# An HGRN2 recurrence with a maxout feed-forward network: the first FFN group begun on half its tokens, and the first loads taken by four tokens and turned by products

## The chip, the cores and the metric

The kernel runs on one core of a Trainium2 chip. The metric is the device time in microseconds. A core has five engines with instruction streams of their own: PE (matrix products, with its weight loads shown apart as PEld), DVE (vector), ACT (scalar), POOL (GpSimd) and SP, which here only issues transfers. ACT issues some transfers too. All data are fp32 on the chip; the weights come as float64 and are rounded on the chip.

## The reference

```python
f = 1.0 / (1.0 + np.exp(-f_logit))
state = np.zeros((B, H, D, D))                 # B 4, H 8, S 768, D 48
for t in range(S):
    state = f[:, :, t, :, None] * state + np.einsum('bhd,bhe->bhde', k[:, :, t], v[:, :, t])
    y[:, :, t] = np.einsum('bhd,bhde->bhe', q[:, :, t], state)
x = y.transpose(0, 2, 1, 3).reshape(B * S, H * D)   # 3072 x 384
h = np.maximum(np.maximum(x @ w1, x @ w2), x @ w3)  # 384 -> 768
return h @ w_out                                    # 768 -> 384
```

## The kernel before

**Units.** The recurrence is cut into 24 units: unit u is chunk u // 2 of 64 time steps for two of the four batches, so it has 128 tokens. Four units make a group of 512 tokens for the FFN, and there are six groups. Inside a unit the recurrence is done by products: with r the decay from a step to the end of the chunk and prod the decay from its beginning, kh = k * r and qh = q * prod; the pairs kh x qh, masked to be causal, times v give the part inside the chunk, and qh times the carried state gives the rest.

**Feature-major layout.** The scans run along time, so f, k and q are needed with the features on the partitions: 48 features of a head padded to DP = 64, two heads (par) on 128 partitions. `load_tokens` (L156) fetches a unit with tokens on the partitions: one transfer for each of the two batches, whose contiguous pieces are one token of one head, 48 floats. `transposed` (L239) turns such a tile by four PE transposes of 128 x 128 against the identity. Units 0 to 7 (BY_ROWS) go this way; later ones come in 32 x 32 blocks that DVE turns (L246), and `pad_blocks` (L140) fills their padding on POOL. The padding holds 40 for f (so the gate is 1) and 0 for k and q.

**The work of a unit.** `sigmoids` (L257) turns f and makes the gate on ACT. `after` (L277) does the first scan (r, L282), a reciprocal, the turn of k and kh (L289). `before` (L294) does the second scan (prod, L296), the turn of q and qh (L300). `carry` (L303) scales the state on POOL. `keys` (L310) turns kh back (L315, copied by ACT at L317), `pairs` (L322) makes the scores (L328) and masks them on DVE (L331), `values` (L335) makes y (L342) and the new state (L351), which DVE adds (L359) or, for units 0 and 1, copies (L357). `finish` (L364) adds the carried part (L372) and ACT copies y into heads (L378). The product tiles of y have one buffer, those of the FFN (`p`) two; the turned k and q of units 0 to 3 also use the `p` buffers.

**The FFN.** `pack` (L382) gathers heads into xT by ten transfers (L389). `ffn` (L394) has 18 steps (six column blocks j, three weight matrices i), each three products of 512 columns (L401) into a `p` tile; the first of three is copied by ACT (L405), the other two go into a running maximum on DVE (L407). Then come four output steps (L422). It is a generator: `fill(n)` runs the next n steps between the parts of the units. A 512-column product shows as two records in the profile.

**Weights.** They come in 24 pieces of 384 KB (18 for the first layer, 6 for the second). A piece is rounded by two ACT operations (`round_begin`, L212 and L215), two on DVE and one on POOL (`round_middle`, L224, L225, L227) and a last on DVE (`round_end`, L234). Three pieces are ended before the first FFN step and the rest during the first group's steps.

**Order.** The order of all instructions is written out by hand (L459 to L583): each engine runs its own in that order, and SP's and ACT's transfers are issued in that order too. Units 0 to 3 come first; after them `busy(14)` (L448), 14 products whose result is not used, stands while xT is packed, and then the first group's FFN is interleaved with units 4 to 7, and so on. At the end, between the eighth and ninth step of the last group, the smallest decay is reduced (L578 to L582) to decide whether a general path must run.

Of the kernel before, what the change touches and what calls it, by code (L numbers as in the profile page):

```python
# [50 lines left out]
GATE_PAD = 40.0  # L51
# [3 lines left out]
def kernel(  # L55
# [32 lines left out]
    def fast():  # L88
        ctx = ExitStack()
        with ctx:  # L90
# [31 lines left out]
            for t in r_tiles:  # L122
                nc.gpsimd.memset(t[:, LEN:], 1.0)
            ones = keep.tile([128, 1], FP32, name="ones")
            nc.vector.memset(ones, 1.0)
# [5 lines left out]
            PADS = {"f": GATE_PAD, "k": 0.0, "q": 0.0}  # L131
            room = {nm: [keep.tile([128, 2 * H * DP], FP32, name=f"{nm}_ld{i}") for i in range(2)] for nm in PADS}
            rows = {nm: [room[nm][u // 2][:, u % 2 * H * DP:(u % 2 + 1) * H * DP].rearrange("t (h d) -> t h d", d=DP)
                         for u in range(4)] for nm in PADS}
            blocks = {nm: [t.rearrange("p (n h d) -> p n h d", n=C // 32, d=32) for t in room[nm]] for nm in PADS}
            for nm, pad in PADS.items():
                for t in rows[nm]:
                    nc.vector.memset(t[:, :, D:DP], pad)

            def pad_blocks(i):  # L140

                for nm, pad in PADS.items():
                    for p0 in (32, 96):
                        yield nc.gpsimd.memset(blocks[nm][i][p0:p0 + 32, :, :, D - 32:], pad)
# [9 lines left out]
            both = (nc.sync, nc.scalar)  # L154

# [6 lines left out]
            def load(u, queues=one, names="fkq"):  # L162
                for nm, src in (("f", f_logit), ("k", k), ("q", q)):
                    if nm not in names:
                        continue
                    if u < BY_ROWS:
# [12 lines left out]
            def load_v(u):  # L179
                load_tokens(v_tiles[u % NLD], v, u)  # L180
# [58 lines left out]
            def transposed(x, name="tr"):  # L239
                t = {"tr": ps_tr, "p": ps_f}[name].tile([128, HP, 128], FP32, name=name)  # L240
                flat = x.rearrange("t h d -> t (h d)")
                for hp in range(HP):
                    nc.tensor.transpose(t[:, hp, :], flat[:, hp * 128:(hp + 1) * 128], ident)  # L243
                return t.rearrange("p h (a t) -> p h a t", a=2)
# [5 lines left out]
            by_pair = lambda t: t.rearrange("p (a h) t -> p h a t", a=2)  # L250
# [6 lines left out]
            def sigmoids(u):  # L257
                gate = gate_tiles[u % 2]
                if u < BY_ROWS:
                    nc.scalar.activation(by_pair(gate)[:, :, :, 1:], transposed(rows["f"][u % 4]), AF.Sigmoid)  # L260
                else:
                    sig = work.tile([128, C // 32, 2 * HP, 32], FP32, name="sig")
                    nc.scalar.activation(sig, block("f", u), AF.Sigmoid)  # L263
                    ready[u] = sig

            def features(nm, u):

                if u < BY_ROWS:
                    t = transposed(rows[nm][u % 4], "p" if u < GRP else "tr")
                    return t.rearrange("p h a t -> p a h t")  # L270
# [6 lines left out]
            def after(u):  # L277
# [7 lines left out]
                nc.vector.reciprocal(from_inv[u % 2][:, :, 0], whole)  # L285
                kt = features("k", u)
# [48 lines left out]
            def values(u):  # L335
# [9 lines left out]
                if u < NU - 2:  # L345
# [10 lines left out]
                    if u < 2:  # L356
                        nc.vector.tensor_copy(new, ds)  # L357
# [24 lines left out]
            def pack(u0, u1, xT, queues=one):  # L382

                t, n = slice(u0 * UT, (u1 + 1) * UT), 0
                for h in range(H):
                    for lo, hi in ((h * D, min(h * D // 128 * 128 + 128, h * D + D)), (h * D // 128 * 128 + 128, h * D + D)):
                        if lo < hi:
                            p0 = h % 2 * DP + lo - h * D
                            queues[n % 2].dma_start(out=xT[lo % 128:lo % 128 + hi - lo, lo // 128, t],  # L389
# [3 lines left out]

            def ffn(g, xT):  # L394
                hm = work.tile([128, NJ, TOK], FP32, name="hm", bufs=1)
                for j in range(NJ):
                    top = None
                    for i in range(3):
                        p = ps_f.tile([128, TOK], FP32, name="p")
                        for kt in range(NK):  # L400
                            nc.tensor.matmul(p, lhsT=w_in[i][:, kt, j * 128:(j + 1) * 128], rhs=xT[:, kt, :],  # L401
                                             start=(kt == 0), stop=(kt == NK - 1))
                        if i == 0:
                            top = work.tile([128, TOK], FP32, name="top")
                            nc.scalar.copy(top, p)  # L405
                        else:
                            nc.vector.tensor_tensor(hm[:, j, :] if i == 2 else top, p, top, op=ALU.max)  # L407

                        if g == 0:
                            step, last = 3 * j + i, 3 * NJ  # L410
                            for r in range(*(3 + (len(pieces) - 3) * n // last for n in (step, step + 1))):
                                round_end(r)
                                if r + 2 < len(pieces):
                                    round_begin(r + 2)
                                    round_middle(r + 2)
                            load_weights(2, r + 1)
                            next(pads, None)
                        yield
                for i in range(GRP):
# [4 lines left out]
                    if g == 0:  # L424
                        next(pads, None)
# [3 lines left out]
                    for a in range(2):  # L429
                        t0 = (2 * bp + a) * S + c * C  # L430
                        nc.sync.dma_start(out=out[t0:t0 + C, :], in_=o[a * C:(a + 1) * C, :])
                    yield
# [18 lines left out]
            pads = iter(())  # L451

# [6 lines left out]
            with tc.manual_schedule():  # L459
                load(0, both)  # L460
                load(1, both, "f")
                load(1, one, "kq")
                load_v(0)
                load(2)
                load(3, one, "f")
                load_v(1)
                load(3, one, "kq")
                load_v(2)
                load_weights(3)
                load_v(3)  # L470
                xT = new_xT()
                sigmoids(0)
                after(0)
                before(0)
                sigmoids(1)
                keys(0)
                after(1)
# [3 lines left out]
                for u in range(2):  # L481
                    values(u)
                    keys(u + 1)
                    after(u + 2)
                    carry(u + 2)
                    pairs(u + 1)
                    busy(1)
                    finish(u)
                    before(u + 2)
                    if u == 0:  # L490
                        sigmoids(3)
                for n in range(2):
                    round_begin(n)
                values(2)
                for n in range(2):
                    round_middle(n)
                keys(3)
                finish(2)
                load_weights(3)
                load(GRP, one, "fk")  # L500
                pairs(3)
                busy(1)
                round_begin(2)
                round_middle(2)
                values(3)
                round_end(0)

                nc.tensor.transpose(ps_tr.tile([128, 128], FP32, name="tr"), ident, ident)
                finish(3)
                round_end(1)  # L510
                round_end(2)
                pack(0, GRP - 1, xT, both)
                for n in range(3, 5):
                    round_begin(n)
                    round_middle(n)
                busy(14)
                load(GRP, one, "q")
                load_v(GRP)
                load_weights(3)
# [3 lines left out]
                fill(1)  # L523
                sigmoids(GRP)
                after(GRP)
                fill(1)
                before(GRP)
                carry(GRP)
                fill(1)
                for u in range(GRP, NU):  # L530
                    n = u + 1
                    fill(0 if u == 2 * GRP else 2 if u % 2 and u > 2 * GRP else 1)
# [21 lines left out]
                    fill(1)  # L554
                    if n < NU:
                        after(n)
                    fill(1)
# [3 lines left out]
                    if n < NU:  # L561
                        before(n)
                        carry(n)
                        if n in (5, 7):
# [240 lines left out]
```

## Time and profile before

| | us |
|---|---|
| median of 6 runs (485.75 to 489.51) | 487.66 |
| the profiled execution | 486.75 |
| its span, first to last instruction | 485.0 |
| PE busy | 464.8 |
| DVE busy | 223.8 |
| ACT busy | 109.2 |
| POOL busy | 99.2 |

Busy times are sums over the span, and the stages have different limits: a table of stages, the waits of one engine and the chain of work that ended last say which engine sets the time where. In the chain, each line gives the start, the length and the engine, tile and line of a piece of work. A timeline line gives the start, the length, the engine, the line, the operation and its tiles, and in brackets the idle time before it with what ended that.

### The profile page before, as it was taken

The numbers are of one execution on the slowest core, as the hardware profiler recorded it, in microseconds if no ns is written. First come the engines' busy times: TensorE is split into PE (matmuls) and PEld (weight loads), VectorE is DVE, ScalarE is ACT, GpSimd is POOL, SyncE is SP. The second block draws the span as 40 slices with busy tenths as digits, with TensorE's granted clock in tenths as the row PEclk, the third lists the DMA queues.
The fourth block names the chain that finished last, engine by engine and source line by source line (L and its number), as shares of the span: only waits on it lengthen the run. The fifth ranks groups of instructions, "written<-read, shape, count | busy, mean of one in ns | idle before, by whom it ended". The sixth has DMA issues, their size and how long they took to land.

```text
span 485.0 us, 10037 instructions
## 1 busy us (share of the span) xinstructions
PE 464.8 (96%) x4101; PEld 251.2 (52%) x4101; DVE 223.8 (46%) x346; ACT 109.2 (23%) x227; POOL 99.2 (20%) x132
## 2 busy tenths in 40 slices
PE   5889999989999999999999999999999999989994
PEld 4665556546545456455546555546554445434452
DVE  7876999984255362264362263362254310112110
ACT  2344445431212202022202122112122102000000
POOL 2122566642121120120120220220211300000000
PEclk9899999999999999999999999999999999999998
DMA  9989999633673042665042664033620012100002
GB/s 129 172 207 206 253 228 199 95 77 72 109 88 53 7 77 49 109 81 77 0 82 53 109 86 66 0 73 61 110 41 1 1 49 50 32 1 1 0 22 50
DMA packets 170007, 38.51 MB, mean 79 GB/s; under 512 B 154976, under 2 KB 168800, under 8 KB 169952
## 3 DMA queue, kind: packets, MB, share of 16 engines
q1 hardware_dynamic: 166208, 36.50, 42.5%
q10 hardware_dynamic: 3744, 1.28, 1.4%
q8 instruction: 34, 0.56, 0.5%
q14 instruction: 21, 0.17, 0.1%
HBM read 28.31 MB, written 4.72 MB: 68 GB/s over the span
## 4 chain that ended last, share of the span: by engine, by line
PE 87%; DVE 3%; SPq 3%; DMA 3%; ACT 1%; issue 1%; POOL 0%; ACTq 0%; DVEq 0%; POOLq 0%
PE p L401 55%; PE p L422 19%; PE y L342 3%; PE y L372 2%; PE a L328 2%; SPq L174 2%; PE y L351 2%; PE tr L315 1%; PE p L448 1%; PE tr L243 1%; DMA f_ld<-in_f_logit_dram 1%; DMA k_ld<-in_k_dram 1%; DVE prod L296 1%; SPq L159 1%; SPq L389 1%
## 5 line engine op out<-in xcount | busy, mean ns | idle before, releaser
L401 PE MATMUL p<-xT,w_in 128*128 128x512 f32 x648 | 288.3, 597 | 1.0 <-ACT top L405 0.7
L401 PEld LDWEIGHTS p<-xT,w_in 128*128 128x128 f32 x648 | 119.9, 190 | 139.0 <-issue 132.7
L422 PE MATMUL p<-w_out,hm 128*128 128x384 f32 x288 | 96.6, 490 | 0.6 <-DVE w_out L234 0.6
L407 DVE TENSOR_TENSOR top<-p,top 128x512 f32<-128x512 f32 x36 | 24.7, 687 | 119.1 <-PE p L401 118.9
L422 PEld LDWEIGHTS p<-w_out,hm 128*128 128x128 f32 x288 | 53.8, 190 | 38.1 <-issue 2.4
L405 ACT COPY top<-p 128x512 f32<-128x512 f32 x36 | 21.1, 585 | 175.8 <-PE p L401 175.8
L407 DVE TENSOR_TENSOR hm<-p,top 128x512 f32<-128x512 f32 x36 | 24.8, 690 | 50.5 <-PE p L401 50.5
L288 POOL COPY ends<-r 128x8 f32<-128x8 f32 x24 | 4.6, 192 | 190.9 <-DVE r L282 190.8
L227 POOL TENSOR_TENSOR top_bits<-top_bits,rest_bits 128x384 uint32<-128x384 uint32 x24 | 28.0, 1167 | 36.9 <-DVE top_bits L225 26.6
L427 ACT COPY o<-p 128x384 f32<-128x384 f32 x24 | 11.4, 476 | 106.3 <-PE p L422 103.1
L296 DVE TENSOR_TENSOR_SCAN prod<-gate,from_inv 128x520 f32<-128x520 f32 x24 | 34.8, 1450 | 0.0
L282 DVE TENSOR_TENSOR_SCAN r<-gate,from_one 128x520 f32<-128x520 f32 x24 | 30.9, 1289 | 2.9 <-issue 2.2
L378 ACT COPY heads<-y 64x256 f32<-64x256 f32 (+1 forms) x72 | 26.5, 369 | 8.8 <-PE y L372 7.6
L331 DVE TENSOR_TENSOR at<-a,mask 128x512 f32<-128x512 f32 x24 | 16.5, 688 | 24.9 <-PE a L328 24.9
L300 POOL TENSOR_TENSOR qh<-qt,prod 128x512 f32<-128x512 f32 x16 | 18.8, 1177 | 37.6 <-DVE qt L247 37.6
L289 POOL TENSOR_TENSOR kh<-kt,r 128x512 f32<-128x512 f32 x16 | 19.8, 1234 | 14.0 <-DVE kt L247 14.0
L342 PEld LDWEIGHTS y<-at,v_ld 64*64 64x64 f32 x768 | 14.0, 137 | 16.5 <-issue 14.4
L317 ACT COPY ks<-tr 128x512 f32<-128x512 f32 x22 | 12.9, 586 | 40.1 <-PE tr L315 39.7
L306 POOL TENSOR_TENSOR state<-st,ends 128x384 f32<-128x384 f32 x22 | 20.3, 925 | 0.2
L247 DVE STREAM_TRANSPOSE gate<-sig 128x512 f32<-128x512 f32 x16 | 11.3, 707 | 17.3 <-ACT sig L263 17.3
L342 PE MATMUL y<-at,v_ld 64*64 64x64 f32 x768 | 17.3, 228 | 1.1 <-ACT top_bits L212 0.9
L328 PE MATMUL a<-qh,kh 48*64 48x64 f32 x768 | 15.7, 219 | 1.4 <-POOL qh L300 1.4
(66 smaller groups left out, 281.6 us busy)
## 6 DMA issues: line engine op xcount, KB each, us to landing
raw<-in_moe_w_dram SPq DMA_DIRECT2D x18, 384.0 KB, 6.1
v_ld<-in_v_dram SPq DMA_DIRECT2D x48, 96.0 KB, 3.1
out_dram<-o SPq DMA_DIRECT2D x48, 96.0 KB, 2.2
raw<-in_moe_w_out_dram SPq DMA_DIRECT2D x6, 384.0 KB, 5.8
xT<-heads SPq DMA_DIRECT2D x30, 72.0 KB, 2.2
f_ld<-in_f_logit_dram SPq DMA_DIRECT2D x32, 64.0 KB, 2.7
k_ld<-in_k_dram SPq DMA_DIRECT2D x32, 64.0 KB, 2.5
q_ld<-in_q_dram SPq DMA_DIRECT2D x32, 64.0 KB, 2.6
```

Of the source, the lines that this page charges most:

```text
L227: nc.gpsimd.tensor_tensor(top, top, rest, op=ALU.add)
L282: nc.vector.tensor_tensor_scan(r[:, 0:LEN][:, ::-1], flat(gate)[:, ::-1], flat(from_one)[:, ::-1], 1.0, op0=ALU.mult, op1=ALU.max)
L289: (nc.vector if u < BY_ROWS else nc.gpsimd).tensor_tensor(kh.rearrange("p h a t -> p a h t"), kt, by_batch(r[:, 1:LEN + 1].rearrange("p (x ...
L296: nc.vector.tensor_tensor_scan(flat(prod), flat(gate_tiles[u % 2]), flat(from_inv[u % 2]), 1.0, op0=ALU.mult, op1=ALU.max)
L306: nc.gpsimd.tensor_tensor(t, states[u % 2], ends[:, u, :].unsqueeze(2).to_broadcast([128, 2 * HP, D]), op=ALU.mult)
L328: nc.tensor.matmul(p[t, par, hp * C:(hp + 1) * C], lhsT=kh[r, hp, a, :], rhs=qh[r, a, hp, :], start=True, stop=True)
L342: nc.tensor.matmul(y[o:o + DP, a, hp * C:(hp + 1) * C], lhsT=v_ld[s, 2 * hp + par, :], rhs=d["at"][s, par, hp, :], start=(hp == 0), stop=F ...
L378: nc.scalar.copy(heads[o, :, t0 + a * C:t0 + (a + 1) * C], y[i, a, 0:HP * C].rearrange("p (h t) -> p h t", h=HP))
L401: nc.tensor.matmul(p, lhsT=w_in[i][:, kt, j * 128:(j + 1) * 128], rhs=xT[:, kt, :], start=(kt == 0), stop=(kt == NK - 1))
L405: nc.scalar.copy(top, p)
L407: nc.vector.tensor_tensor(hm[:, j, :] if i == 2 else top, p, top, op=ALU.max)
L422: nc.tensor.matmul(p[:, 0:DM], lhsT=hm[:, j, i * UT:(i + 1) * UT], rhs=w_out[:, j, :], start=(j == 0), stop=(j == NJ - 1))
```

## The change

Units 0 to 3 are loaded with four consecutive tokens of a head on a partition, so a contiguous piece has 4 x 48 floats and one transfer serves both batches; SP and ACT take them in turn. The partition order is (token block, batch, pair of heads). Such a tile is turned by eight products of the data (128 partitions, 64 columns) with the identity, one for each of four token positions and two heads of a pair, written into PSUM with a step of four elements. The padding then holds other data instead of 40 or 0; only 48 rows of each half are used, and the final test of the decays counts feature rows only (`is_feature`). `pad_blocks` is gone.

```diff
+                    if u < GRP:
+                        c, bp = divmod(u, 2)
+                        queues[NAMES.index(nm) % 2].dma_start(
+                            out=slots[nm][u][:, 0:H * D].rearrange("p (par e) -> p par e", par=2),
+                            in_=src[2 * bp:2 * bp + 2, :, c * C:(c + 1) * C, :].rearrange(
+                                "b (h par) (tb t) d -> tb (b h) par (t d)", par=2, t=4))
...
+                if u < GRP:
+                    t = {"tr": ps_tr, "p": ps_f}[name].tile([128, 2 * HP, C], FP32, name=name)
+                    for n in range(4):
+                        for par in range(2):
+                            e0 = (par * 4 + n) * D
+                            nc.tensor.matmul(t.rearrange("p x (tb t) -> p tb x t", t=4)[par * DP:(par + 1) * DP, :, :, n],
+                                             lhsT=slots[nm][u][:, e0:e0 + DP],
+                                             rhs=ident.rearrange("p (tb x) -> p tb x", x=2 * HP), start=True, stop=True)
+                    return by_batch(t)
```

The FFN of group 0 takes its first two column blocks (J_HALF) in half steps of 256 tokens: six half steps on units 0 and 1, then the same six on units 2 and 3, then full steps. xT of group 0 is packed in two halves of ten transfers each, the first right after unit 1. `busy(14)` is gone. A full step now yields twice, a half step once, and the counts of `fill` are about doubled. The rounding of the weights follows a new formula: one piece a half step at first.

```diff
+                steps = [(j, slice(0, TOK)) for j in range(NJ)]
+                if g == 0:
+                    steps = [(j, slice(n * HALF, (n + 1) * HALF)) for n in range(2) for j in range(J_HALF)] + steps[J_HALF:]
...
+                            n_step += 1
+                            ahead = n_step + 2 if n_step <= 6 else 8 + (2 * n_step - 11) // 3 if n_step <= 12 else n_step
+                            for r in range(done, min(ahead, len(pieces))):
                                 if r + 2 < len(pieces):
                                     round_begin(r + 2)
-                                    round_middle(r + 2)
-                            load_weights(2, r + 1)
-                            next(pads, None)
+                                if r + 1 < len(pieces):
+                                    round_middle(r + 1)
+                                round_end(r)
+                                done = r + 1
+                            load_weights(2, done)
                         yield
+                        if w == TOK:
+                            yield
```

The order of the opening changes: `scan` (the first scan and the reciprocal) is split from `after` and stands earlier on DVE; the loads are reordered, with nine pieces of weights instead of six before the first pack; the state copy of units 0 and 1 goes from DVE to ACT; two pieces of weights are ended before the FFN instead of three.

```diff
                 load(0, both)
-                load(1, both, "f")
-                load(1, one, "kq")
+                load(1, (nc.scalar, nc.sync))
                 load_v(0)
-                load(2)
-                load(3, one, "f")
+                load(2, one, "f")
                 load_v(1)
-                load(3, one, "kq")
+                load(2, one, "kq")
+                load_weights(3)
+                load(3)
                 load_v(2)
                 load_weights(3)
                 load_v(3)
+                load_weights(3)
...
+                values(1)
+                finish(1)
+                pack(0, 1, xT, one, 0)
+                load(GRP, one, "f")
+                before(2)
+                sigmoids(3)
+                keys(2)
+                scan(3)
+                after(3)
+                carry(3)
+                pairs(2)
+                busy(1)
...
                 finish(3)
-                round_end(1)
-                round_end(2)
-                pack(0, GRP - 1, xT, both)
-                for n in range(3, 5):
-                    round_begin(n)
-                    round_middle(n)
-                busy(14)
+                pack(2, 3, xT, (nc.sync, nc.scalar, nc.sync, nc.scalar, nc.sync), 1)
+                load_weights(1)
+                load(GRP, one, "k")
+                load_weights(2)
                 load(GRP, one, "q")
                 load_v(GRP)
-                load_weights(3)
                 load(GRP + 1)
                 load_v(GRP + 1)
                 pending.append(ffn(0, xT))
-                fill(1)
+                fill(6)
                 sigmoids(GRP)
+                scan(GRP)
                 after(GRP)
-                fill(1)
+                fill(2)
```

In the loop over units 4 to 23 each `fill(1)` becomes `fill(2)`, but the last one of a unit is `fill(1)` for units below 8, that is half of a full step. At the end the reductions are issued three steps ahead of the product that counts their result:

```diff
-                fill(8)
+                fill(12)
 
                 least = work.tile([128, 1], FP32, name="least")
                 nc.vector.tensor_reduce(out=least, in_=ends.rearrange("p u a -> p (u a)"), op=ALU.min, axis=AX.X)
                 nc.vector.tensor_scalar(least, least, P_MIN, None, op0=ALU.is_lt)
+                fill(6)
                 n_low = ps_tr.tile([1, 1], FP32, name="tr")
-                nc.tensor.matmul(n_low, lhsT=least, rhs=ones, start=True, stop=True)
+                nc.tensor.matmul(n_low, lhsT=least, rhs=is_feature, start=True, stop=True)
```

## The prediction

> **What bounds the kernel now.** I read the table of stages first, then the waits of PE, then the chain that ended last, then the timeline of the opening. The columns of the stages are the stretch, its length, the busy time (instructions) of PE, PEld, DVE, ACT and POOL, the granted clock, DMA share and GB/s.
>
> ```profile
> 5.00:10.00 5.00, 4.21 (x18) 3.09 (x17) 3.38 (x5) 0.77 (x2) 0.19 (x1) 1.00 1.52 152
> 10.00:15.00 5.00, 3.44 (x54) 2.66 (x55) 4.86 (x7) 1.03 (x3) 0.19 (x1) 0.90 1.53 153
> ...
> 20.00:25.00 5.00, 4.50 (x115) 3.45 (x113) 4.86 (x8) 2.19 (x5) 1.02 (x2) 1.00 0.93 248
> ...
> 70.00:80.00 10.00, 10.00 (x94) 5.31 (x92) 9.76 (x19) 3.89 (x9) 6.55 (x8) 1.00 1.06 285
> ...
> 200.00:300.00 100.00, 100.00 (x936) 52.47 (x935) 42.70 (x59) 20.95 (x43) 16.69 (x20) 1.00 0.49 74
> ```
>
> From about 43 us on PE is full, so time can be won only in the first 40 us and in PE's few later gaps (engine, line, waited for, us, times, longest):
>
> ```profile
> PE tr L243 <- DMA f_ld<-in_f_logit_dram: 6.5, 3, 4.7
> PE a L328 <- POOL qh L300: 1.4, 1, 1.4
> PE tr L581 <- DVE least L579: 1.3, 1, 1.3
> ...
> PE p L422 <- DVE w_out L234: 0.6, 1, 0.6
> ```
>
> The chain (start, us, what) shows the opening:
>
> ```profile
> 9.33 4.41 DMA f_ld<-in_f_logit_dram
> 13.88 1.02 PE tr L243 x4
> ...
> 32.16 0.66 PE y L372 x32
> 32.82 6.24 PE p L448 x28
> 39.06 0.86 PE p L401 x2
> 40.25 1.96 PE p L401 x4
> 42.20 0.87 PE tr L243 x8
> 43.08 2.58 PE p L401 x6
> ```
>
> The f of unit 2 lands only at 13.88. From there DVE and PE alternate to the end of unit 3's last products, 32.82, which I call F. Then the 28 records of L448 warm the clock and compute nothing, while ACT and SP issue the ten transfers of xT:
>
> ```profile
> 34.06 3.44 ACTq L389 DMA_DIRECT2D xT<-heads  x5
> ...
> 37.55 0.56 ACT L212 ACTIVATE top_bits<-raw 128x384 f32<-128x384 f32 x1 [3.52 <-DMA xT<-heads]
> ```
>
> ACT computes nothing while it issues: 0.69 us for each of five.
>
> **Loads by four tokens.** Twelve transfers of 192 KB in 256 pieces of 768 B take the place of 24 of 96 KB in 512 pieces of 192 B. At 0.65 us an issue, 12 x 0.65 = 7.8 us of queue time go. At 10 to 15 us, mostly 192 B pieces, the table has 153 GB/s at a share of 1.53; at 20 to 25, with weight rows among them, 248 GB/s at 0.93. A tensor's 192 KB then takes 0.8 to 1.3 us. Unit 0's f lands at 4.67 now, with only its other half beside it. After, k runs beside it on ACT's queue, so I bound its landing by 3.9 and 5.0 and take 4.4. SP then issues f2 as its sixth transfer, near 4.5 us, and f2 lands near 9, long before its turn. Moved: nine pieces of weights instead of six are issued before the first pack, three of them now past f, k, q of unit 3. That costs unit 3 up to 3.2 us of SP (3.22 us for three L200 at 24.73); it lands by about 19 and is needed at 21, so nothing is lost; without that cover it would be what exceeds 21. The early pack (ten issues, 6.5 us) and unit 4's f stand on SP from 21.7 to 30, where nothing else waits until F. Group 0 thus has 20 pack transfers instead of ten, the first ten hidden.
>
> **Products instead of transposes.** Now four records of 128 columns turn a tensor: eight in 0.87 us back to back, 0.109 each. After, eight products with two records each, 16 records, on 64 columns of the array, writing PSUM four elements apart. No row has this form. In sequence it is 16 x 0.109 = 1.74 us. If the two halves of the array run together it is 0.87. The rows nearest are the 64 x 64 products: 32 records of 64 columns would be 1.74 in sequence; L342 takes 0.62 (2.8 of 4 at once), L328 0.47 (3.7 of 4). At 70 to 93% of two at once I get 1.24 to 0.94, and take 1.0, since the columns are longer. The bounds stay 0.49 (packed like L328) and 1.74. Early ones cost double: the first four transposes take 1.08 against 0.43 in the stream. On warm PE it is 12 x (1.0 - 0.43 to 0.59), about 5.5 us more work where PE had slack.
>
> The Trainium skill, "TensorE: Matmul & The Clock Gate", Part 3, says that a weight load overlaps running matmuls only when its row group differs, and these products use all rows. The trace disagrees for whole-array loads: L448 runs 28 records of 256 columns in 6.24 us, 0.223 each, against 0.215 for half of a 512-column record, each with its load. By the rule, 16 loads of 0.14 (L243) would add 2.2 us a tensor and the time would be near 507; by the row, nothing.
>
> **The opening, walked.** DVE per unit, start to start (17.36 to 21.84): scan 1.26, reciprocal 0.12, kh 0.56, mask 0.6, scan 1.3, qh 0.6; the state copy of 0.55 goes to ACT for units 0 and 1. PE per unit: keys 0.6, pairs 0.5, values 1.1, finish 0.65, three turns. With f0 at 4.4: turned at 6.4 (cold), sigmoid 7.05, scan from 7.1 (6.48 now). PE turns k0 to 8.3, q0 to 10.0, f1 to 11.1; then keys, k1 and pairs of unit 0 to 13.2, q1 14.2, f2 15.2; values 0 to 16.3, keys and pairs 1 to 17.4, k2 18.4, values 1 from 18.85 to 19.95, q2 20.95, f3 21.95, keys 2 22.5, k3 23.5, pairs 2 24.0, q3 25.5, values 2 26.6. DVE waits for q2 (0.65) and f3's gate (1.05) and ends qh of unit 3 at 27.15 (26.88 now). Then the chain is state 0.55, finish 2, pairs 3, mask, values 3, state 0.55, finish 3: 4.95 us (6.0 now, where unit 2's heads and weight rounding stood in ACT's way). F is 32.1: **0.7 won**. The bounds: with turns of 0.49, DVE's 4.5 us a unit bounds and F is 29.5; with 1.74 in sequence the same walk gives F = 40.1.
>
> **Half the tokens.** From F the old kernel ends three full steps (18 records) at 48.67, less 1.30 of transposes between: F + 14.55. After, six half steps of 6 x 0.223 = 1.34 us start at F, 8.0 if nothing waited. But ACT copies heads until F + 1.2 and issues four of the second pack, 4 x 0.69, until F + 4.0; only then comes the copy of step 1's PSUM, and with two PSUM buffers step 3 waits until F + 4.4. Behind the four issues ACT also has the rounding of piece 4 (0.95), which DVE's pair (0.72), POOL (1.0) and then DVE's last op (0.5) follow. Step 4 waits for piece 3 until F + 6.6, step 5 for piece 4 until F + 8.1, and the sixth ends at F + 10.8. SP's six issues end near F + 5.9 and land by F + 8, before step 7, the first to read the second half. The other six half steps cost 6 x (1.34 - 1.29) = 0.3. **Won: 14.55 - 10.8 - 0.3 = 3.45.** The bounds are 6.2 (no step waits) and 0 (the whole of it waits).
>
> **Behind it.** 22 pieces less 6 are left after the sixth step, two fewer than now, where DVE is at 98%; the POOL memsets of 12 x 0.52 are gone too. I price both at nothing, PE being full there already. The doubled counts give the same 19 steps before unit 8, but the first output step now comes ahead of unit 7's values, so none stands between these and unit 8's keys. After values: state 0.65, scan 1.23, turn 0.69, POOL 1.18, then pairs: 3.9 us, of which PE fills 1.25. That is 2.65 of waiting against 0.55 + 1.41 now: **0.7 lost**; the bounds are 1.96 won (no wait left) and 1.9 lost (DVE late by as much as one scan, 1.23, more).
>
> **The tail.** PE stops at 427.88 and runs at 429.33 for the single L581. The reductions now stand three steps (7.7 us) ahead of it: **1.45 won**, less nothing, since DVE is idle there.
>
> **The sum.** 0.7 + 3.45 - 0.7 + 1.45 = 4.9. The profiled execution took 486.75, its span 485.0 and 1.75 around it: 486.75 - 4.9 = 481.85. The median of the runs, 487.66, lies 0.91 above it, so I add half and say 482.3, own range 478.5 to 486.
>
> **Rivals.** First, the turns run one after the other or the PSUM stride slows them: F = 40.1 instead of 32.1, 8.0 lost, 490.3, slower. It decides from a warm turn of about 1.45 us, since 0.74 us more in each of the twelve cost 8.0 and 4.9 is to be had. For it: no row has two column halves sharing all rows. Against: the 64 x 64 rows beat what two row halves alone would give (0.87 for 32 records). Second, the half start starves: ACT's issues and the rounding stretch the six steps to F + 14.5, 3.45 goes, 485.7. For it: ACT's 3.52 us wait behind the pack in the fence above. Third, the opening becomes DVE's: turns below 0.6, F near 29.5, 2.6 more, 479.7. For it: DVE has 4.86 of 5 us at 10 to 15 and 20 to 25. Against: PE has 4.50 beside it.
>
> **Numbers.** Forecast 0.55, first rival 0.19, second 0.12, third 0.14. A measurement here can tell 0.5% from no change, 485.2 to 490.1. Faster: 0.52 of the forecast, all 0.14 of the third, 0.04 of the second: 0.70. Within: 0.03 of the forecast, 0.06 of the second, and 0.05 of the first, which lies at the edge: 0.14. Slower: 0.14 of the first and 0.02 of the second: 0.16. The range 477.5 to 489 leaves out most of the first rival and the third's lower edge.
>
> **What would show it.** The 16-record turns at about 1.0 us warm; F near 32; no L448 run of 28, and half-step records of 0.22 us from F with a wait on ACT's copy before the third; a PE wait of some 2.6 us before unit 8's pairs; no wait on L581's successor. I am wrong if a warm turn takes 1.5 us or more, or if first full steps start no earlier than now.

## The result, and the profile after

| | before | after |
|---|---|---|
| median of the runs, us | 488.50 | 492.41 |
| ratio to before (95% interval) | | 1.008 (1.0062 to 1.0097) |
| span of the profiled execution, us | 485.0 | 490.6 |

The change makes the kernel 0.8% slower; 482.3 us and a gain were forecast. The medians differ by 3.9 us and the two traced spans by 5.6, since the old kernel's profiled execution (486.75 us) was 1.75 below its median. Three places that both traces have tell where the 5.6 went: the start of unit 3's last products, of unit 8's pairs, and of unit 9's pairs.

| start, us | before | after | lost so far | forecast |
|---|---|---|---|---|
| last products of unit 3 | 32.16 | 34.77 | 2.6 | 0.7 won |
| pairs of unit 8 | 109.54 | 113.54 | 4.0 | 3.4 won |
| pairs of unit 9 | 131.90 | 138.82 | 6.9 | 3.4 won |
| end of the span | 485.0 | 490.6 | 5.6 | 4.9 won |

So 2.6 us were lost in the opening, 1.4 in the stage of the half start (which was to win 3.45, less 0.7 at unit 8), and 2.9 between two pairs further on, where nothing had been expected. Only the tail did as forecast and gave 1.3 back. PE's waits of the profile after in its first 60 us (engine, tile, line, what it waited for; us, times, longest):

```profile
PE p L442 <- ACT top L447: 1.5, 1, 1.5
PE p L442 <- DVE top L449: 1.3, 1, 1.3
PE a L349 <- issue: 1.3, 1, 1.3
PE p L442 <- DVE hm L449: 1.2, 1, 1.2
PE p L442 <- DVE w_in L243: 0.9, 2, 0.5
...
PE tr L256 <- issue: 0.6, 1, 0.6
```

L442 are the FFN's first products, half steps among them: 4.9 us of waits where the old kernel had 0.3, besides its 6.24 us of unused products. The wait on L581's successor at the end is gone. The two "issue" rows are waits for which the profile shows no releaser; I call them holes. In the chain of the profile after they stand in the opening, and further down stands the low clock:

```profile
16.52 0.59 PE tr L336 x4
17.36 1.27 issue
18.63 0.68 PE a L349 x25
...
112.31 1.18 POOL qh L321
113.54 1.13 PE a L349 x32
114.67 10.43 PE p L468 x24
```

The pairs of unit 8 take 1.13 us instead of 0.69, and 24 records of the output steps 10.43 instead of 7.94. The stages around it give the clock (stretch, length, busy time and instructions of PE, PEld, DVE, ACT and POOL, granted clock, DMA share, GB/s):

```profile
110.00:112.00 2.00, 1.25 (x36) 0.94 (x36) 2.00 (x3) 0.77 (x2) 0.43 (x1) 1.00 0.43 59
112.00:114.00 2.00, 0.46 (x16) 0.47 (x20) 0.23 (x1) 0.91 (x3) 1.69 (x2) 0.71 0.00 0
114.00:116.00 2.00, 2.00 (x30) 1.31 (x23) 0.69 (x1) 0.00 (x0) 0.27 (x1) 0.50 0.20 42
116.00:118.00 2.00, 2.00 (x5) 1.05 (x4) 1.18 (x2) 0.63 (x1) 0.00 (x0) 0.50 0.71 100
118.00:120.00 2.00, 2.00 (x5) 1.16 (x4) 1.56 (x3) 0.00 (x0) 0.45 (x2) 0.58 0.68 97
```

In the first two rows PE is busy 1.25 and 0.46 of 2 us each, and from about 113 to 119 us the granted clock is 0.50. Before the change it stayed at 1.00 through a similar hole:

```profile
108.00:110.00 2.00, 0.59 (x40) 0.46 (x32) 0.17 (x1) 1.26 (x4) 1.68 (x2) 1.00 0.29 32
110.00:112.00 2.00, 2.00 (x23) 1.27 (x15) 0.69 (x1) 0.00 (x0) 1.31 (x3) 1.00 0.10 26
```

### The profile page after: what moved, and what is told of

Same layout as the page of the kernel before. It is cut to its first block, busy times and chain, and to the rows that moved or that the text cites. A ratio compares the mean times of both kernels' runs of the same rounds, so it can differ in the third digit from the quotient of the medians.

```text
span 490.6 us, 10333 instructions
## 1 busy us (share of the span) xinstructions
PE 467.7 (95%) x4255; PEld 259.3 (53%) x4255; DVE 220.9 (45%) x341; ACT 110.4 (23%) x231; POOL 96.0 (20%) x124
## 4 chain that ended last, share of the span: by engine, by line
PE 88%; DVE 6%; issue 2%; DMA 1%; ACT 1%; ACTq 1%; POOL 0%; DVEq 0%; POOLq 0%
PE p L442 54%; PE p L468 19%; PE y L363 3%; PE a L349 3%; PE y L393 2%; PE y L372 2%; PE tr L336 2%; PE p L256 1%; DVE r L299 1%; DVE top_bits L233 1%; DVE prod L317 1%; DVE w_in L243 1%; DMA f_ld<-in_f_logit_dram 1%; PE tr L256 1%; PE tr L262 1%
## 5 line engine op out<-in xcount | busy, mean ns | idle before, releaser
L442 PE MATMUL p<-xT,w_in 128*128 128x512 f32 (+1 forms) x684 | 289.9, 575 | 5.6 <-ACT top L447 2.1
L442 PEld LDWEIGHTS p<-xT,w_in 128*128 128x128 f32 x684 | 126.3, 190 | 140.0 <-issue 125.1
L468 PE MATMUL p<-w_out,hm 128*128 128x384 f32 x288 | 98.8, 499 | 0.0
L449 DVE TENSOR_TENSOR top<-p,top 128x512 f32<-128x512 f32 (+1 forms) x38 | 25.1, 660 | 125.2 <-PE p L442 123.9
L468 PEld LDWEIGHTS p<-w_out,hm 128*128 128x128 f32 x288 | 55.2, 194 | 38.9 <-issue 5.2
L447 ACT COPY top<-p 128x512 f32<-128x512 f32 (+1 forms) x38 | 21.4, 563 | 182.3 <-PE p L442 179.7
L449 DVE TENSOR_TENSOR hm<-p,top 128x512 f32<-128x512 f32 (+1 forms) x38 | 25.2, 663 | 51.2 <-PE p L442 51.1
L471 ACT COPY o<-p 128x384 f32<-128x384 f32 x24 | 11.4, 476 | 107.0 <-PE p L468 103.8
L299 DVE TENSOR_TENSOR_SCAN r<-gate,from_one 128x520 f32<-128x520 f32 x24 | 32.2, 1341 | 6.1 <-issue 3.4
L317 DVE TENSOR_TENSOR_SCAN prod<-gate,from_inv 128x520 f32<-128x520 f32 x24 | 34.1, 1419 | 0.0
L327 POOL TENSOR_TENSOR state<-st,ends 128x384 f32<-128x384 f32 x22 | 21.9, 997 | 0.2
L380 DVE TENSOR_TENSOR st<-y,state 128x384 f32<-128x384 f32 x20 | 11.1, 557 | 16.0 <-PE y L372 15.8
```

Of the source, the lines that this page charges most:

```text
L299: nc.vector.tensor_tensor_scan(r[:, 0:LEN][:, ::-1], flat(gate)[:, ::-1], flat(from_one)[:, ::-1], 1.0, op0=ALU.mult, op1=ALU.max)
L317: nc.vector.tensor_tensor_scan(flat(prod), flat(gate_tiles[u % 2]), flat(from_inv[u % 2]), 1.0, op0=ALU.mult, op1=ALU.max)
L327: nc.gpsimd.tensor_tensor(t, states[u % 2], ends[:, u, :].unsqueeze(2).to_broadcast([128, 2 * HP, D]), op=ALU.mult)
L442: nc.tensor.matmul(p if g or w < TOK else p.rearrange("p (two t) -> p two t", two=2), lhsT=w_in[i][:, kt, j * 128:(j + 1) * 128], rhs=rhs, ...
L449: nc.vector.tensor_tensor(hm[:, j, t] if i == 2 else top, p, top, op=ALU.max)
L468: nc.tensor.matmul(p[:, 0:DM], lhsT=hm[:, j, i * UT:(i + 1) * UT], rhs=w_out[:, j, :], start=(j == 0), stop=(j == NJ - 1))
```

## The experiments

All ratios are to the kernel before, measured beside each run. "Distance A" is the start of unit 4's pairs less that of unit 3's last products (24.6 us after the change; before it 19.45 with two steps fewer in between, so 19.45 + 2 x 2.58 = 24.6 for equal work). "Distance B" is the start of unit 9's pairs less that of unit 8's: 22.4 before, 25.3 after. "Unit 3's last" is the start of unit 3's last products; these three come from one profiled execution of each run.

| run | median, us | ratio (95% interval) | unit 3's last | A | B |
|---|---|---|---|---|---|
| e1, products ahead of unit 8's pairs | 490.90 | 1.0048 (1.0024 to 1.0072) | 36.04 | 24.6 | 22.4 |
| e2, no half steps | 494.42 | 1.0132 (1.0080 to 1.0185) | 36.68 | 24.0 | 22.4 |
| e3, second pack on SP alone | 493.97 | 1.0122 (1.0071 to 1.0173) | 36.29 | 24.8 | 25.3 |
| e4, loads and turns as before | 495.23 | 1.0154 (1.0102 to 1.0205) | 34.61 | 28.6 | 24.1 |
| e5, loads and turns alone | 488.26 | 0.9981 (0.9948 to 1.0014) | 33.82 | | 22.4 |
| e6, weights early, else as before | 494.44 | 1.0125 (1.0083 to 1.0168) | 39.66 | | 22.4 |
| e7, output step behind unit 7's values | 491.53 | 1.0049 (1.0014 to 1.0084) | 35.91 | 24.6 | 24.0 |
| e8, the tail alone | 487.46 | 0.9966 (0.9932 to 1.0000) | 32.88 | | 22.4 |
| e9, six pieces of weights later | 494.78 | 1.0106 (1.0045 to 1.0167) | 37.71 | 26.1 | 24.1 |
| e10, six pieces not rounded | 488.61 | 1.0000 (0.9970 to 1.0031) | 33.93 | 22.9 | 24.1 |
| e11, three small edits of before | 486.37 | 0.9946 (0.9918 to 0.9974) | 32.76 | | 22.4 |
| e12, and the scans earlier | 485.95 | 0.9942 (0.9916 to 0.9967) | 33.17 | | 22.4 |
| e13, all nine pieces later | 494.73 | 1.0110 (1.0010 to 1.0210) | 37.17 | 27.4 | 24.1 |

### e1: keep PE busy through the hole at unit 8

```diff
+                    if u == 2 * GRP:
+                        busy(4)
                     pairs(u)
```

> The changed kernel with four products (eight records of 256 columns, 1.8 us) whose result is not used, ahead of unit 8's pairs. Nothing is reordered; the wait of PE for POOL's qh (1.8 us) stays, but PE works in it. Theory A, that the granted clock of 0.50 from 113 to 119 us costs as much as the wait itself (10.43 us for 24 L468 records against 7.94, and 1.13 against 0.62 for pairs): the clock stays at 1.00 and the kernel takes 2.5 to 3 us less. Rival B, that the clock fell for another reason or only in this execution: less than 1 us either way.

In the timeline of PE (start, us, engine, line, tiles) of this run the wait is filled and the clock holds:

```profile
112.94 1.99 PE L493 MATMUL p<-from_one,ident 128*128 128x256 f32 x8
114.87 0.69 PE L349 MATMUL a<-qh,kh 48*64 48x64 f32 x32
115.49 8.01 PE L468 MATMUL p<-w_out,hm 128*128 128x384 f32 x24
```

By the local measure theory A holds: 8.01 instead of 10.50 for the same 24 records, and distance B falls from 25.3 to 22.4, the 2.9 us that were lost there. The median falls by 1.5 us, between the two theories, and the intervals of this run and of the changed kernel (1.0062 to 1.0097) overlap. Distance B in the table shows why that can be: with the same hole it is 25.3 in e3, 24.0 or 24.1 in e4, e7, e9 and e10, and 22.4 in e2. The time lost there differs from one profiled execution to the next.

### e7: the output step back behind unit 7's values

```diff
                     if n < NU:
                         scan(n)
                         after(n)
-                    fill(2)
+                    fill(0 if u == 2 * GRP - 1 else 2)
...
-                    fill(1 if u < 2 * GRP else 2)
+                    fill(3 if u == 2 * GRP - 1 else 1 if u < 2 * GRP else 2)
```

> The changed kernel with the first output step of group 0 issued after unit 7's values again instead of ahead of them. Theory A, that the place of this step opens the wait ahead of unit 8's pairs (0.7 us for kh and 1.8 us for qh) and so the low clock behind it: both shrink by 1.5 us or more, the clock stays at 1.00 and the kernel takes 2 to 4 us less than the changed one. Rival B, that DVE is the one that is late: the wait only moves to the second output step, and less than 1 us is won.

Rival B: PE still waits 1.7 us for qh and 0.4 for kh (1.8 and 0.7), and the median falls by 0.9. Against the start of unit 3's last products, DVE's first scan stands where it stood (72.0 us behind it in both). The state addition (L380) comes 0.9 us earlier, but the second scan (L317), which now starts beside POOL's kh (110.38, 1.18 us), takes 2.06 us instead of 1.23, so unit 8's pairs come only 0.1 us earlier.

### e2: no half steps

```diff
-            J_HALF = 2
+            J_HALF = 0
...
-                            ahead = n_step + 2 if n_step <= 6 else 8 + (2 * n_step - 11) // 3 if n_step <= 12 else n_step
+                            ahead = 2 + (22 * n_step + 17) // 18
...
+                busy(14)
                 load_weights(1)
```

> The changed kernel without half steps: J_HALF 0, the 14 unused products back while the second half of xT is packed, and the pieces of weights ended evenly over 18 full steps. Theory A, that the half start gained nothing because ACT, DVE and POOL pace it: within 1 us of the changed kernel, with unit 4's pairs at the same distance from the end of unit 3 (24 us). Rival B, that it did gain what was forecast and something else lost more: 2.5 to 4 us slower than the changed kernel.

By the local measure theory A holds: distance A is 24.0 without half steps and 24.6 with them. The half start won nothing there; it lost half a microsecond. That place itself varies, though: the 28 records of unused products take 6.3 us in before, e2, e5 and e6, but 7.6 to 8.2 in e8, e11 and e12, where the clock was low (0.50 from 32 to 36 us in e8), and there distance A is 20.5 to 21.2; with 5.16 for the two steps, the half start would have won 1.1 to 1.8 us over those. The kernel as a whole is 2.0 us slower than the changed one, between the two theories. The traces put that elsewhere: this run's unit 3 is 1.9 us later, with an opening hole of 2.1 us instead of 1.3, and its rounding, spread over 18 steps, stands on DVE at unit 7, where PE waits 0.9 us for the state and 1.5 for qh (0.9 for qh alone in the changed kernel) and the clock is 0.50 behind it.

### e3: ACT freed of the second pack

```diff
-                pack(2, 3, xT, (nc.sync, nc.scalar, nc.sync, nc.scalar, nc.sync), 1)
+                pack(2, 3, xT, one, 1)
```

> The changed kernel with all ten transfers of the second half pack on SP, so that ACT issues none after unit 3. Theory A, that ACT's four issues (2.55 us) delay the whole chain of rounding behind them: the first copy of a half step comes 2.5 us earlier, PE's wait of 1.5 us for it goes, and the kernel is 1.5 to 2.5 us faster. Rival B, that DVE and POOL's rounding at 1.94 us a piece is what paces the half steps: the wait moves to DVE's last operation of a piece and at most 0.7 us is won; SP's ten issues may then be late for step 7.

PE's waits from 36 to 62 us in this run:

```profile
PE tr L262 <- DMA k_ld<-in_k_dram: 2.1, 1, 2.1
PE p L442 <- DVE w_in L243: 1.6, 4, 0.5
```

Rival B, as for the first part: the 1.5 us on ACT's copy and both waits on DVE's maxima are gone, and in their place come four waits on the last rounding operation, and one of 2.1 us on unit 4's k, whose load stands behind the ten issues on SP. Distance A is 24.8. One wait was exchanged for others.

### e10: without the rounding of six pieces

```diff
+                    if n < 6:
+                        src = q.rearrange("b h s d -> (b h s d)")[n * 49152:(n + 1) * 49152].rearrange("(r c) -> r c", c=128)
-                    if src.dtype != FP32:
+                    elif src.dtype != FP32:
```

> The changed kernel without the rounding of the first six pieces: their places in w1, w2 and w3 are filled straight from q, so the output is not the reference's; all products and copies stay. Theory A, that the rounding (1.94 us a piece on DVE and POOL together) and not ACT's issues or the two PSUM buffers paces the half steps: unit 4's pairs come 19 to 21 us after unit 3's last products instead of 24.6. Rival B, that PSUM copies behind ACT and DVE's other work pace them: 23 us or more.

This run leaves part of the rounding out, so its output is another. Distance A is 22.9: the rounding is worth 1.7 us there, and neither theory holds alone. What is left from 34 to 62 us is ACT's issues, DVE's order and later loads:

```profile
PE p L444 <- ACT top L449: 1.5, 1, 1.5
PE p L444 <- DVE hm L451: 1.2, 1, 1.2
PE tr L264 <- DMA q_ld<-in_q_dram: 0.6, 1, 0.6
```

How rounding paces DVE is seen in the changed kernel's timeline of DVE, where a piece is ended every 1.95 us:

```profile
42.73 0.56 DVE L243 SCALAR_TENSOR_TENSOR w_in<-raw,top_bits 128x384 uint32<-128x384 uint32 x1
43.21 1.16 DVE L233 TENSOR_SCALAR top_bits<-top_bits 128x384 f32<-128x384 f32 x1
44.40 0.36 DVE L234 TENSOR_SCALAR top_bits<-top_bits 128x384 uint32<-128x384 uint32 x1
44.68 0.55 DVE L243 SCALAR_TENSOR_TENSOR w_in<-raw,top_bits 128x384 uint32<-128x384 uint32 x1
```

L233 takes 1.16 us here and 0.35 when POOL is idle; POOL's addition for the piece before runs from 42.96 for 1.19 us.

### e4 and e5: the loads and the turns

e4 takes the loads by four tokens and the products out of the changed kernel; e5 puts them alone, with the padding that goes with them, into the kernel before.

```diff
-                    if u < GRP:
-                        c, bp = divmod(u, 2)
-                        queues[NAMES.index(nm) % 2].dma_start(
...
-                    elif u < BY_ROWS:
+                    if u < BY_ROWS:
                         load_tokens(rows[nm][u % 4], src, u, queues)
```

> The changed kernel with the loads of units 0 to 3 by single tokens and the PE transposes as before the change, all else as changed. Theory A, that products cost the opening PE time (0.85 to 1.02 us a tensor warm against 0.44) and two holes of 1.27 us without a releaser, from 288 more PE instructions: no such holes, and unit 3 ends 2 to 4 us earlier than 35.5 unless its loads come late. Rival B, that the late loads cost as much as the products (the f of unit 2 landed at 13.88 before the change): the end of unit 3 within 1 us of 35.5.

> The kernel before with only the loads by four tokens, their turning by products and the padding that goes with these; its order of work, full steps and places of the weights stay, and the POOL memsets of the padding go. Theory A, that the holes of 1.3 to 2.1 us in PE's stream at about its 440th instruction come from fetching instructions while the weights' transfers fill the DMA queues: the weights start at 20 us here, so no hole above 0.5 us there, and unit 3 ends 0.5 to 2.5 us before the 32.8 of the kernel before, since f of unit 2 no longer lands at 13.88; 486 to 488. Rival B, that the holes come from the products' 288 more instructions: a hole of 1 us or more at the same count, and no gain or a loss.

e4: the last products of unit 3 start at 34.6 and end at 35.3, within 1 us of 35.5, so rival B: loads and turns together neither win nor lose in the opening. The hole is there too, 1.56 us at the same count of PE's instructions (loads and products), now inside other products. This run then loses 4 us in distance A, since SP's longer queue delays the first half pack and PE waits 2.6 us for xT. e5: no change of the time (0.9981, 0.9948 to 1.0014). A hole of 1.13 us is there, so the first half of theory A fails as put; its premise failed as well, as the twelve fewer issues brought the weights forward to 12.5 us. The products themselves took what was forecast, as PE's timeline of e5 shows, 16 records in 1.98 us at first and about 1.0 later:

```profile
4.94 1.98 PE L254 MATMUL tr<-ident,f_ld 128*64 128x128 f32 x16 [4.94 <-DMA f_ld<-in_f_logit_dram]
...
16.46 0.44 PE L254 MATMUL p<-ident,k_ld 128*64 128x128 f32 x4
18.03 0.88 PE L254 MATMUL p<-ident,k_ld 128*64 128x128 f32 x12 [1.13 <-issue]
```

The hole cuts a group of 16 records after the fourth. All of them read one loaded tile and write one tile, so neither data nor another engine is a likely cause.

### e6, e9 and e13: where the holes come from

e6 issues nine pieces of weights early in the kernel before. e9 and e13 issue six and nine of them later in the changed kernel, behind transfers of the first half pack. The edit of e9:

```diff
                 load_v(2)
-                load_weights(3)
                 load_v(3)
-                load_weights(3)
...
                             n += 1
+                            if half == 0 and n in (1, 2):
+                                load_weights(3)
```

> The kernel before with its first nine pieces of weights issued early, three after the loads of unit 2, three after v of unit 1 and three after v of unit 2; transposes and all else as before. Theory A of the holes: a hole of 1 us or more without a releaser at about PE's 440th instruction, which the kernel before does not have. Rival B: no hole; only later loads of unit 3. In both, the later data of units 1 to 3 may move the end of unit 3 by 0 to 3 us, so the hole and not the time tells.

> The changed kernel with its second and third three pieces of weights issued behind the first and second transfer of the first half pack (about 25 us) instead of at 14.5 and 20.8 us; nothing else moves. Theory A, that PE's holes without a releaser (1.3 to 2.1 us at about its 440th instruction, 0.3 to 0.6 at its 670th) come from the weights' transfers in flight: both holes below 0.5 us, unit 3 ends at 32 to 33.5 instead of 35.4 to 36.7, and the kernel takes 1.5 to 3 us less than the changed one. Rival B, that they come with the instruction stream itself: holes as before, same time.

> The changed kernel with all nine early pieces of weights issued behind the first, second and third transfer of the first half pack (about 25 us). The transfers of f, k, q and v should then be through by about 15 us. Theory A, that PE's hole at about its 440th instruction, near 17 us, comes from transfers in flight shortly before it: the hole is below 0.5 us. Rival B, that this place in the stream always stalls, whatever the transfers: 1.2 us or more, as in every run of the changed order so far. The time itself grows by some us in both, since the first three pieces are late for their rounding.

e6 cannot tell: PE stands 3.35 us on f and 1.94 on k of later units at that place, so a hole could not show. It shows something else: weights moved ahead of data that the opening still needs cost 7.5 us there (39.66 against 32.16). In e9 the second hole, at 23.7 us, is gone, and a new one of 2.2 us stands where the weights now are:

```profile
16.72 0.33 PE L349 MATMUL a<-qh,kh 48*64 48x64 f32 x4
18.54 0.68 PE L349 MATMUL a<-qh,kh 48*64 48x64 f32 x28 [1.49 <-issue]
...
33.88 0.20 PE L372 MATMUL y<-v_ld,ks 64*64 64x48 f32 x1
36.29 0.68 PE L372 MATMUL y<-v_ld,ks 64*64 64x48 f32 x31 [2.21 <-issue]
```

That the hole at 23.7 us is gone proves little, since e2, e4, e7 and e10 have none there either, with these weights where they were. The new hole is what speaks for theory A: 2.2 us in e9 and 2.3 in e13, each just behind the moved weights. The first hole stays, 1.49 us in e9 and 1.35 in e13, from 16.52 to 17.86. Rival B as put fails too: the kernel before passes the same count of instructions near 21.0 us without a hole.

The traces show what PE stood for, since they keep the transfers of instructions. The queue's row before and after the change (packets, MB, share):

```profile
q8 instruction: 34, 0.56, 0.5%
...
q8 instruction: 35, 0.57, 0.5%
```

A packet has 16 KB, and 35 of them go with 8621 records of PE and its loads, so each holds about 250 of them. The fifteen traces have sixteen holes of 0.3 us or more ahead of the end of unit 3, and all stand at one of four counts, 256 apart: the 450th, 706th, 962nd and 1218th record. In the order of time, the first packet of this queue belongs to the first of these places, the second to the second, and so on:

| run, count | packet, us | PE goes on | after the packet's end |
|---|---|---|---|
| after, 450 | 16.09 to 17.31 | 18.63, hole of 1.27 | 1.3 |
| after, 706 | 21.16 to 22.24 | 23.77, hole of 0.60 | 1.5 |
| e5, 450 | 14.77 to 16.32 | 18.03, hole of 1.13 | 1.7 |
| e4, 450 | 19.10 to 20.26 | 21.79, hole of 1.56 | 1.5 |
| e9, 1218 | 33.79 to 34.92 | 36.29, hole of 2.21 | 1.4 |
| e13, 450 | 14.99 to 16.45 | 17.86, hole of 1.35 | 1.4 |
| before, 450 | 16.91 to 18.43 | 21.03, no hole | 2.6 |
| before, 706 | 21.96 to 23.64 | 25.97, no hole | 2.3 |

In no trace does PE pass such a place earlier than 1.3 us after the end of its packet, and each of the sixteen holes ends 1.3 to 1.7 us after it. So PE stood for its next instructions; the kernel before comes to the same places later, when they are there. Other transfers can make a packet late: in e9, with 378 GB/s in flight from 32 to 34 us (64 in the changed kernel), the packet for the 1218th record starts 3.9 us after PE passed the 962nd, and 0.7 us after in the changed kernel. For the first hole e13 does not decide this, because the loads were still in flight while its packet came (DMA share 1.42 from 14 to 16 us); which transfers hold that packet up stays open.

In both runs the time grew (1.0106 and 1.0110): the new hole delays the start of unit 3's last products to 37.7 and 37.2, and distance A is 1.5 and 2.8 us longer.

### e8, e11 and e12: what is worth keeping

e8 is the kernel before with the tail of the change. e11 adds two edits that are not of the change; e12 adds the change's earlier scans and its state copies on ACT.

```diff
-                            step, last = 3 * j + i, 3 * NJ
+                            step, last = 3 * j + i, 3 * NJ - 1
...
+                load(2, one, "f")
                 load_v(0)
-                load(2)
+                load(2, one, "kq")
...
-                fill(8)
+                fill(6)
...
+                fill(3)
                 n_low = ps_tr.tile([1, 1], FP32, name="tr")
```

> The kernel before with only the last part of the change: the reductions of the smallest decay issued three steps ahead of the product that counts their result. PE's wait of 1.45 us (427.88 to 429.33) goes. Theory A: 1.2 to 1.5 us less than before, 0.25 to 0.3%. Rival B, that another wait takes its place at the end: no difference.

> The kernel before with the reductions three steps ahead at the end, the last piece of weights ended one step earlier, and f of unit 2 loaded ahead of v of unit 0. Expected: 1.45 us from the end, up to 0.8 us in the opening (f of unit 2 at 12.5 to 13 instead of 13.88) and up to 0.8 us at unit 8 (no DVE rounding behind the last full step): 2 to 3 us less than before. If the opening is bound by DVE after all, 1.4 to 2.

> As the run beside it, and the first scan of units 2 and 3 ahead of the values of units 0 and 1 on DVE, and their state copies on ACT, as in the change. If DVE's order holds the opening, unit 3 ends 1 to 2 us earlier than in the run beside it; if PE and the loads hold it, no difference.

e8: the chain near its end now runs through, with 0.12 us where 1.45 had been:

```profile
417.23 15.45 PE p L401 x36
432.68 0.12 PE tr L582 x2
432.79 31.10 PE p L401 x72
```

The median is 1.15 us less than that of the runs beside it, with an interval that reaches 1. e11 beats both kernels: 486.37, 0.9946 (0.9918 to 0.9974). Of the waits of PE at unit 8, the one for the last piece (0.6) is gone and the one for qh is 1.2 instead of 1.4; the opening did not gain, since k and q, and then v, came late in turn for the f that came early (1.7 us on q). e12 is no better than e11 within their intervals: DVE's order was not what held the opening.

## Why the prediction was wrong

**Loads and turns: right.** A turn was taken at 1.0 us warm and 2.0 cold and is 0.87 to 1.09 and 1.95 to 1.98. The two halves of the array do run together, though all rows are shared (in the trace after, the records of a warm turn start in pairs, 6 to 7 ns apart, a pair every 0.109 us), so the first rival, the only one on the slow side, is not what happened; the time came near its 490.3 by another way. The rule of the Trainium skill ("TensorE: Matmul & The Clock Gate", Part 3) that weight loads overlap only for other row groups does not agree with these runs: 16 loads of 0.137 us and 16 products fit into 0.87 to 1.09 us. f0 landed at 4.9 instead of 4.4, the upper part of its bounds.

**The opening: wrong by 3.3 us** (32.1 forecast, 35.4 measured for the end of unit 3). The step that failed is the walk of PE, which let its products follow each other whenever data were there. The first scan starts at 7.62, 0.5 late; the first hole takes 1.27, so pairs of unit 1 end at 19.25 instead of 17.4; after the second PE is 2.9 late. The old trace has no row for such a wait in the opening, so no term stood for it. In its place the traces show PE waiting for packets of its own instructions: with earlier data and eight products a tensor it reaches the 450th record at 17.36 us instead of 21.03, but that record's packet ends only at 17.31, and PE goes on 1.3 us after it. The moving of the weights was priced at nothing with unit 3's loads as the only thing queued behind them; these packets can be held up too (e9).

**Half the tokens: wrong by its whole 3.45 in the profiled executions.** The first six half steps ended 11.5 us after unit 3's last product (10.8 forecast), with the waits in the order given: ACT's copy first, then pieces at 1.95 us each. The failing step is the next one, that the other six half steps cost 0.3: with the four transposes' 0.4 they should have taken 8.5 us and took 11.4, from 47.62 to 59.0, since their maxima stand on DVE behind a first scan of 2.04 us, a second of 1.70 (1.24 and 1.23 at unit 8, where POOL is idle beside them) and more rounding (1.3 and 1.2 us of waits). So the second rival's ground was right and its place too small. e2 shows the sum to be nil by distance A, or up to 1.8 us against the old order's executions with a low clock there; e10 gives the rounding 1.7 of it, and e3 that taking ACT's part away alone wins nothing.

**Behind it: half right.** The wait ahead of unit 8's pairs was forecast at 2.65 and is 0.7 + 1.8 = 2.5. What the sum left out is the clock: 0.50 for some 6 us, 2.9 us in the profiled execution by its longer records, and gone in e1, where PE works through the wait. The old wait of 0.55 + 1.41 had not set it off, and the step priced a longer wait as only so much longer. How much it costs is partly chance: with the same wait it was nothing in e2 and 1.6 to 2.9 us elsewhere.

**The tail: right**, 1.3 to 1.45 us in the traces, 1.15 between medians in e8.

## What to carry to other kernels

A part of the order that fills idle PE time is worth its length only if the engines that feed it have that time too: here a half step used up a new piece of weights in 1.34 us of products, where a full step has 2.58, and DVE, ACT and POOL brought one every 1.95 us. Price a wait of PE with what the clock does behind it, not by its length alone. When transfers are moved forward or PE gets more instructions early, look at the packets of instructions in that stretch too, and test a reordered opening by the place of one late event in several runs, since the size of the first hole moves from 1.3 to 2.1 us with the same opening.

## What the runs showed that was not expected

- PE's stream can stand for 0.3 to 2.3 us inside a group of products while its next 16 KB of instructions come. In the changed order it does so at about the 450th record of PE and its loads in every run, whichever line that is. After such a hole the clock fell as well in e1 (0.53 from 20 to 22 us). Both make the opening differ from run to run: unit 3's last products start at 34.8 to 36.7 in runs with the same opening.
- The clock fell to 0.50 after a stretch in which PE was busy 1.7 of 4 us with short products, and came back after some 6 us of dense work. A run with the same wait kept it (e2).
- A DVE operation of 0.35 us takes 1.16 us beside POOL's addition of 1.19 us, and a scan of 1.23 us takes 2.06 beside POOL's kh (e7).
